# DMAs of the attention exchange and of two stored w2 combinations issued by GpSimd instead of SyncE, and one store moved behind the exchange

## The chip, the cores and the metric

The kernel runs as one program on one core of a Trainium2 chip. The metric is the device time of an execution in microseconds; less is better. Three executions of the kernel before took 1772.20, 1772.83 and 1773.43 us, so the median is 1772.83 us.

## The reference

Three layers follow one another on 2304 tokens of 512 features. Everything is float32.

```python
# 1. attention inside chunks of 64 tokens: 4 batches, 8 heads, 576 tokens, 64 features a head
scores = (q_c @ k_c^T) / 8;  attn = softmax(scores);  x = attn @ v_c      # x: [2304, 512]
# 2. a mixture of 8 dense experts, weighted by a gate that is normalised 8 times by rows and columns
P = exp(x @ w_gate - max);  8 times: P /= row sums;  P /= column sums;  P *= 2304 / 8
out = sum over e of P[:, e] * (relu(x @ w1[e]) @ w2[e])                   # w1[e]: [512, 1024]
# 3. an MLP with three up projections
h = max(out @ w1, out @ w2, out @ w3)                                     # 512 -> 768
result = h @ w_out                                                        # 768 -> 512
```

## The kernel before

The tokens are cut into 18 tiles of 128, and these into three super-blocks of six tiles. A matrix product is done by a scheme of Strassen's kind: seven products of 384 columns stand for eight, and every operand is split into a high and a low part, so that a product is six matmuls. ACT casts the high part; POOL or DVE subtracts it to get the low part (`hilo`, L272 and L273).

**Items.** The work is a list of items. Items 0 to 31 are the mixture's layer on the first super-block: item n is a slice of 256 hidden units, with its own up weights (w1) and down weights (w2), which it reads raw from HBM, combines and splits (`prep`, `prep_x`). The later items take the combined weights back from HBM, where items 0 to 31 have stored them (`keep`: `w1s` for the up weights, `w2s` for the down weights). So only items 0 to 31 issue the DMAs that the change touches, and they end about 570 us into the span.

Inside an item the code walks through seven positions, one for each product (`up`), and hangs the other work on them: `at(n, pos, ...)` registers a step, `early` one that comes ahead of the rest. Each engine runs its instructions in the order in which they are written; nothing is reordered.

**What item n does to the w2 weights.** `prep(n, 2)` casts the raw tile `sw` and splits one half (L273, 128x512, into `wr`). `prep_x` makes two combinations on DVE (L193 to L197). The first, x, is cast by ACT (L203) and completed by DVE (L210); the second, y, is cast by ACT and its low part is subtracted by POOL (L272, L273 into the tile `w2y`). Up to item 14 x and y have one buffer each, in use by every item; later the items alternate between two (`w2z`). So the cast of item n's y waits until the store of item n-1's y has landed. `keep(n, 2)` stores x (L221) and `keep(n, 3)` stores y (L223), 512 KB each, in item n+1 at position 0. That makes 64 such stores.

**The exchange.** Items 1 to 13 also carry the attention of the last twelve tiles. Scores (L804) are matmuls at position 0 of an item; their softmax follows, DVE transposes blocks of 32 (L865, tile `eT`), and `att_swap` (L869) completes the transpose: ACT copies `eT` to `aT` (L872), then four DMAs of 32 partitions and 32 KB exchange blocks between partitions (L876). In the next item PE multiplies `aT` by v (L905, tile `xp`) right behind the next scores, and between them in some items the gate (L922). That makes 48 such DMAs.

**POOL** has in each item: four sums for the next item's up weights (`ws`, L128 to L131), their low parts (L273: 128x768 and 128x1024 into `wr`), the low part of the item's own w2 (128x512), that of y (128x512), and one of the hidden values (`hr`, L301).

**SP** issues every DMA of the kernel before, in the written order. Where an instruction waits, what is behind it waits too.

Of the kernel before, what the change touches and what calls it, by code (L numbers as in the profile page):

```python
# [33 lines left out]
NPAIR = E * F // 256  # L34
# [18 lines left out]
def kernel(ctx: ExitStack, tc: tile.TileContext, qk, vv, wg, wts, wts2, out):  # L53
    nc = tc.nc
# [55 lines left out]
    def own(n):  # L110

        return n < NPAIR

    def raw1(n):
        if n <= NPAIR:
            g = n % NPAIR
            st[n] = rp.tile([P, 4, 256], F32, name="st", tag="st", bufs=2)
            nc.sync.dma_start(out=st[n][:, 1:3].rearrange("p i f -> p (i f)"), in_=wts[2 * g, :, 0])
            nc.sync.dma_start(out=st[n][:, 0::3], in_=wts[2 * g + 1, :, 0].rearrange("p (i f) -> p i f", i=2))

    def raw2(n):
        if own(n):
            sw[n] = rp.tile([P, 2, 512], F32, name="sw", tag="sw")
            nc.sync.dma_start(out=sw[n], in_=wts[2 * n:2 * n + 2, :, 1].rearrange("c p d -> p c d"))

    def strassen_w(v, s, eng):
        tt = eng.tensor_tensor
        tt(out=s[0], in0=v[0], in1=v[3], op=ALU.add)  # L128
        tt(out=s[1], in0=s[0], in1=v[1], op=ALU.subtract)
        tt(out=s[2], in0=v[1], in1=v[0], op=ALU.subtract)  # L130
        tt(out=s[3], in0=v[2], in1=s[1], op=ALU.subtract)  # L131

    sums, sw2 = {}, {}
# [7 lines left out]
    def prep_sums(n):  # L141
        s = sums[n] = rp.tile([P, 4, 256], F32, name="ws", tag="ws")
        strassen_w([st[n][:, i] for i in range(4)], [s[:, i] for i in range(4)], nc.gpsimd)
# [29 lines left out]
    def prep_x(n, step):  # L173

        if not own(n):
            return
        q = lambda c, a: sw[n][:, c].rearrange("p (f a k r) -> p a k f r", a=2, k=2, f=4)[:, a]
        o = lambda x: x.rearrange("p (k f r) -> p k f r", k=2, f=4)
        tt = nc.vector.tensor_tensor
        if step == 0:  # L180
            if n:
                p = wk.tile([P, 2, 256], F32, name="xw", tag="wk")
            else:
                p = ar[:, TS - 2].rearrange("p (a b) -> p a b", a=2)
            s = rp.tile([P, 2, 256], F32, name="w2c", tag="w2c")
            sw2[n] = (p, s)
            for a in range(2):
                nc.scalar.copy(out=o(p[:, a]), in_=q(0, a))
        elif step == 1:
            p, s = sw2[n]  # L190
            w = w2b(n)[:, 0:2]
            if n:
                tt(out=w[:, :, 1], in0=p, in1=w[:, :, 0].bitcast(F32), op=ALU.subtract)  # L193
            tt(out=o(s[:, 0]), in0=q(1, 1), in1=o(p[:, 1]), op=ALU.add)
            tt(out=o(p[:, 1]), in0=q(0, 0), in1=o(p[:, 1]), op=ALU.subtract)
            tt(out=p[:, 0], in0=s[:, 0], in1=p[:, 0], op=ALU.subtract)
            tt(out=o(s[:, 1]), in0=q(1, 0), in1=o(p[:, 0]), op=ALU.subtract)  # L197
            sw.pop(n)
        elif step == 2:
            p, s = sw2[n]  # L200
            x = w2x(n)
            sums["x", n] = x
            nc.scalar.copy(out=x[:, :, 0], in_=p)  # L203
            y = w2z[0][:, 2:4] if w2z and n % 2 else rp.tile([P, 2, 2, 256], F32R, name="w2y", tag="w2y")
            sums["y", n] = y
            hilo(y[:, :, 0], y[:, :, 1], s)
        else:
            p, s = sw2.pop(n)
            x = sums["x", n]
            tt(out=x[:, :, 1], in0=p, in1=x[:, :, 0].bitcast(F32), op=ALU.subtract)  # L210

    def keep(n, step):
        f32 = lambda x: x.bitcast(F32).rearrange("p s h f -> p s (h f)")
        w2o = w2s[n // 2, :, :, n % 2] if own(n) else None
        if step == 0:
            nc.sync.dma_start(out=w1s[n % NPAIR], in_=f32(w1b(n)))
        elif step == 1:
            nc.sync.dma_start(out=w2o[:, 0:1], in_=f32(w2b(n)[:, 0:1]))
            nc.sync.dma_start(out=w2o[:, 5:7], in_=f32(w2b(n)[:, 2:4]))
        elif step == 2:  # L220
            nc.sync.dma_start(out=w2o[:, 2:4], in_=f32(sums.pop(("x", n))))  # L221
        else:
            nc.sync.dma_start(out=w2o[:, 1:5:3], in_=f32(sums.pop(("y", n))))  # L223


    chunks, slot_of = [], {}
# [44 lines left out]
    def hilo(h, l, v, eng=None):  # L271
        nc.scalar.copy(out=h, in_=v)  # L272
        (eng or nc.gpsimd).tensor_tensor(out=l, in0=v, in1=h.bitcast(F32), op=ALU.subtract)  # L273
# [237 lines left out]
    def fold_all():  # L511
        jobs = [(e, t) for e in (0, NRAW - 1, *range(1, NRAW - 1)) for t in range(TS)]
        loads = [j for j in jobs if j[0] != NRAW - 1]
        got = {}

        def load():
            if loads and len(got) < 6:
                e, t = loads.pop(0)
                got[e, t] = big[0].tile([P, DM], F32, name="u", tag="ld", bufs=6)
                nc.sync.dma_start(out=got[e, t], in_=up_part[e, t])  # L520

        for _ in range(5):
            load()
        yield
        for e, t in jobs:
            load()
            if e == 0:
                nc.scalar.activation(out=ar[:, t], in_=got.pop((e, t)), func=AF.Copy, scale=Pt[:, t, e:e + 1])
            else:
                u = spare[0][:, t] if e == NRAW - 1 else got.pop((e, t))  # L530
                nc.vector.scalar_tensor_tensor(out=ar[:, t], in0=u, scalar=Pt[:, t, e:e + 1],
                                               in1=ar[:, t], op0=ALU.mult, op1=ALU.add)
            yield
# [6 lines left out]
    def x_load(k):  # L540
        kind, sb = phases[k]
        if k == 1:
            xf = spare[0].rearrange("p t d -> p (t d)").rearrange("p (i a w) -> p i a w", a=2, w=W)
            T = lambda i: (xf[:, (1, 3, 4, 6).index(i)] if i in (1, 3, 4, 6) else
                           big[0].tile([P, 2, W], F32, name=f"xf{i}", tag=f"xf{i}"))
        else:
            T = lambda i: bg_[:, :7 * 2 * W].rearrange("p (i a w) -> p i a w", a=2, w=W)[:, i]
        xst.update({i: T(i) for i in range(7)})
        for i, (q, h) in {5: (1, 0), 0: (0, 0), 2: (1, 1), 1: (0, 1)}.items():
            for j in range(TS // 2):  # L550
                t, o = sb * TS + 2 * j + q, xst[i][:, :, j * P:(j + 1) * P]
                nc.sync.dma_start(out=o, in_=(xs if kind == "M" else ys)[t, :, 2 * h:2 * h + 2])
                yield
# [314 lines left out]
    def att_swap(t):  # L868
        eT = et_t.pop(t)  # L869
        aT = ap_.tile([P, 2, H, 32], F32, name="aT", tag="aT")  # L870
        at_t[t] = aT
        nc.scalar.copy(out=aT, in_=eT)  # L872
        for c in range(2):
            for i in range(2):
                src, dst = 64 * c + 32 * i, 64 * c + 32 * (1 - i)
                nc.sync.dma_start(out=aT[dst:dst + 32, i], in_=eT[src:src + 32, 1 - i])  # L876

    def raw_of(t):
        if t // 2 not in raw_t:
# [121 lines left out]
    def at(n, pos, fn):  # L1001
        bg.setdefault((n, pos), []).append(fn)

    for m in range(NT - NPE):
        t, n = NPE + m, 1 + m
        at(n, 1, lambda t=t: (att_norm(t), att_T(t)))
        if m:
            early[n, 2] = lambda t=t: att_swap(t)
        else:
            at(n, 2, lambda t=t: att_swap(t))  # L1010
        at(n + 1, 2, lambda t=t: x_save(t))
    for n in range(1, NT - NPE + 3):
        early[n, 0] = lambda n=n: att_slot(n)
    n = NT - NPE + 2
# [3 lines left out]
    for i in range(SINK_ITERS):  # L1018
        a = 7 * (n + 1 + i // 2)
# [43 lines left out]
    at(n, 0, att_close)  # L1063
    for g in range(NPAIR):
        for s_, (a, b) in enumerate(((0, 2 * (0 < g <= NT - NPE)), (0, 6) if g else (1, 0), (1, 0), (1, 0))):
            if (g, s_) != (1, 0):
                at(g + a if g or s_ else NPAIR, b, lambda g=g, s_=s_: keep(g if g or s_ else NPAIR, s_))
    decs, folds = [decode_all(i) for i in range(2)], fold_all()

    def decode_step(n):  # L1070
# [9 lines left out]
    for k in range(1, 4):  # L1080
        n0 = first_of[k]
        g = x_load(k)
# [6 lines left out]
        for pos in range(7):  # L1089
            a = 7 * (n0 - 1) + (pos + 1 if k == 1 else (0, 1, 2, 7, 7, 7, 8)[pos])  # L1090
            b = 7 * (n0 - 1) + (pos + 2 if k == 1 else (1, 2, 3, 7, 7, 8, 9)[pos])
# [3 lines left out]
    for k in (4, 5):  # L1095
        for j in range(TS // 2):
            n = first_of[k - 1] + 3 * j
            if k == 4 and j < 2:
                n = first_of[3] + 3 + j
# [17 lines left out]
    with tc.manual_schedule():  # L1117
# [60 lines left out]
                next(xg)  # L1178
        for product in part[3:]:
            product()  # L1180
        keep(1, 0)
        raw1(2)
        next(xg)
        w2 = w2_first()
# [12 lines left out]
        prep_x(0, 0)  # L1197
        prep_x(0, 1)
        raw2(1)
        prep_sums(2)  # L1200
        prep_x(0, 2)
        prep_x(0, 3)
        hps.close()
        psum = lambda name, n: pool(name, n, space=bass.MemoryType.PSUM, reuse_waits="tile")
# [110 lines left out]
```

## Time and profile before

| | |
|---|---|
| median of three runs | 1772.83 us |
| the profiled execution | 1774.31 us, its span 1772.5 us |
| PE busy | 1761.9 us (99%) |
| DVE, ACT, POOL busy | 1298.8, 777.1 and 997.5 us |
| chain that ended last | PE 94%, DMA 2%, DVE 1%, ACT 1%, issue 1% |
| granted TensorE clock | 1.0 in all 40 slices |
| DMA queues that moved data | one for all of the kernel's DMAs: 206336 packets, 530.97 MB |

A busy time is the sum over the instructions of an engine. The chain is followed back from the last instruction to what released each step. Times in timelines count from the start of the span. Item 1 begins at 34 us (its scores, L804), item 2 at 53, item 3 at 71, item 4 at 89, item 5 at 107, item 6 at 124 us.

### The profile page before, as it was taken

The page shows a single profiled execution, that of the slowest core. Times are in us where ns is not written, and L with a number is a line of the kernel's source. Part 1 is how long each engine was busy: PE and PEld are TensorE (multiplying, and loading weights), DVE is VectorE, ACT ScalarE, POOL GpSimd, SP SyncE. Part 2 cuts the span into 40 slices and gives each one's busy share as a digit, 9 for nine tenths or more (in the row PEclk, how much of TensorE's full clock was granted, in tenths as well). Part 3 has the DMA queues.
Part 4 walks back from the last instruction along what each step waited for, and adds up shares of the span by engine and source line. Part 5 has one row for each costly group of instructions (what it writes and reads, how often), then busy time and mean ns, then how long its engine had stood idle before and what let it go on. Part 6 is the DMA issues. An engine that isn't in the chain of part 4 may idle for free.

```text
span 1772.5 us, 30171 instructions
## 1 busy us (share of the span) xinstructions
PE 1761.9 (99%) x10764; PEld 1683.4 (95%) x10764; DVE 1298.8 (73%) x2342; ACT 777.1 (44%) x1566; POOL 997.5 (56%) x891
## 2 busy tenths in 40 slices
PE   8999999999999999999999999999999999999999
PEld 7888888998989999999999999999999999999998
DVE  8767667678876787887886887878787766664535
ACT  6665664655555534333333434334333333323221
POOL 4665665767777866666675667576766555000000
PEclk9999999999999999999999999999999999999999
DMA  8999998899988998988889779888988786877662
GB/s 284 317 353 366 340 347 311 321 373 340 357 309 333 334 322 273 333 299 306 279 314 318 257 257 346 306 295 295 318 306 316 265 303 241 283 259 255 243 246 105
DMA packets 206486, 532.89 MB, mean 301 GB/s; under 512 B 16160, under 2 KB 95360, under 8 KB 181248
## 3 DMA queue, kind: packets, MB, share of 16 engines
q1 hardware_dynamic: 206336, 530.97, 84.0%
q8 instruction: 85, 1.39, 0.3%
q14 instruction: 65, 0.53, 0.1%
HBM read 373.31 MB, written 156.02 MB: 299 GB/s over the span
## 4 chain that ended last, share of the span: by engine, by line
PE 94%; DMA 2%; DVE 1%; ACT 1%; issue 1%; POOL 0%; SPq 0%; DVEq 0%; ACTq 0%; POOLq 0%
PE pa L353 28%; PE dn L411 27%; PE dn L469 18%; PE pg L353 14%; PE pb L353 7%; DMA w2s<-w2y 1%; DMA upart<-ar 0%; PE xp L905 0%; PE s L804 0%; DMA qk<-in_qk 0%; PE gp L922 0%; DVE e L830 0%; DVE hs L827 0%; DVE hs L819 0%; DVE nm L818 0%
## 5 line engine op out<-in xcount | busy, mean ns | idle before, releaser
L353 PE MATMUL pa<-xh,wr 128*128 128x384 f32 x1808 | 529.2, 337 | 0.0
L469 PE MATMUL dn<-wr,hr 128*128 128x512 f32 x1476 | 356.2, 392 | 0.0
L353 PEld LDWEIGHTS pa<-xh,wr 128*128 128x128 f32 x1808 | 332.7, 188 | 5.2 <-DVE c L366 0.8
L469 PEld LDWEIGHTS dn<-wr,hr 128*128 128x128 f32 x1476 | 275.4, 188 | 53.9
L353 PE MATMUL pa<-xl,wr 128*128 128x384 f32 x904 | 303.2, 335 | 0.0
L411 PE MATMUL dn<-hr,wr 128*128 128x384 f32 x1344 | 274.8, 335 | 0.0
L353 PE MATMUL pg<-xh,wr 128*128 128x384 f32 x904 | 268.3, 337 | 0.1
L360 ACT COPY s<-pa 128x384 f32<-128x384 f32 x244 | 117.3, 481 | 300.1 <-PE pa L353 276.5
L411 PEld LDWEIGHTS dn<-hr,wr 128*128 128x128 f32 x1344 | 236.9, 188 | 0.1
L366 DVE TENSOR_TENSOR c<-pb,s 128x384 f32<-128x384 f32 x82 | 45.7, 557 | 203.0 <-PE pb L353 180.1
L273 POOL TENSOR_TENSOR hr<-c,hr 128x384 fp32r<-128x384 f32 x96 | 111.1, 1163 | 142.2 <-ACT hr L272 137.0
L411 PE MATMUL dn<-hx,wr 128*128 128x384 f32 x840 | 182.8, 338 | 0.0
L353 PEld LDWEIGHTS pa<-xl,wr 128*128 128x128 f32 x904 | 169.7, 188 | 4.0
L353 PEld LDWEIGHTS pg<-xh,wr 128*128 128x128 f32 x904 | 166.5, 188 | 1.9 <-DVE tq L322 0.4
L353 PE MATMUL pg<-xl,wr 128*128 128x384 f32 x452 | 151.1, 334 | 0.0
L411 PEld LDWEIGHTS dn<-hx,wr 128*128 128x128 f32 x840 | 150.9, 188 | 0.0
L273 POOL TENSOR_TENSOR hr<-tq,hr 128x384 fp32r<-128x384 f32 x128 | 148.4, 1175 | 0.5 <-ACT hr L272 0.5
L353 PE MATMUL pb<-xh,wr 128*128 128x384 f32 x452 | 134.1, 337 | 0.0
L420 DVE TENSOR_TENSOR ar<-dn,ar 128x384 f32<-128x384 f32 x240 | 123.0, 546 | 9.5 <-PE dn L411 9.1
L273 POOL TENSOR_TENSOR hx<-c,hx 128x384 fp32r<-128x384 f32 x60 | 68.8, 1150 | 106.0 <-ACT hx L272 105.5
L411 PE MATMUL dn<-hy,wr 128*128 128x384 f32 x504 | 111.1, 336 | 0.0
L420 DVE TENSOR_TENSOR ax<-dn,ax 128x384 f32<-128x384 f32 x180 | 93.2, 550 | 18.2 <-PE dn L411 18.2
(246 smaller groups left out, 3210.8 us busy)
## 6 DMA issues: line engine op xcount, KB each, us to landing
wr<-w2s SPq DMA_DIRECT2D x80, 1024.0 KB, 6.4
w1s<-wr SPq DMA_DIRECT2D x32, 1792.0 KB, 9.7
wr<-w1s SPq DMA_DIRECT2D x53, 1024.0 KB, 7.2
wr<-w1s SPq DMA_DIRECT2D x58, 768.0 KB, 6.4
w2s<-wr SPq DMA_DIRECT2D x55, 512.0 KB, 6.5
wr<-w2s SPq DMA_DIRECT2D x52, 512.0 KB, 7.1
wr<-scr SPq DMA_DIRECT2D x22, 1024.0 KB, 5.1
wr<-scr SPq DMA_DIRECT2D x27, 768.0 KB, 5.8
```

The costliest lines, as they stand in the source:

```text
L273: (eng or nc.gpsimd).tensor_tensor(out=l, in0=v, in1=h.bitcast(F32), op=ALU.subtract)
L353: nc.tensor.matmul(ps, lhsT=wt[:, x, ws], rhs=y[:, xi, k], start=b not in begun, stop=k == 1 and i == 2, skip_group_check=True)
L360: nc.scalar.copy(out=s[pos], in_=ps)
L366: nc.vector.tensor_tensor(out=inner, in0=ps, in1=s[other], op=ALU.add)
L411: nc.tensor.matmul(p, lhsT=w[:, a, dt * P:(dt + 1) * P], rhs=h[m][:, b], start=m == 0 and q == 0, stop=m == 1 and q == 2)
L420: nc.vector.tensor_tensor(out=o, in0=p, in1=o, op=ALU.add)
L469: nc.tensor.matmul(o, lhsT=h[:, hi, ts], rhs=w, start=(f == 0 and i == 0), stop=(f == 1 and i == 2))
```

## The change

The DMAs of `keep(n, 2)`, `keep(n, 3)` and `att_swap` are issued by GpSimd (POOL) and no longer by SP. The store of item 1's up weights, `keep(1, 0)`, leaves the prologue and is registered like the others, at position 2 of item 1, behind `att_swap`. In the prologue `prep_x(0, 2)`, which casts x and y of item 0 and subtracts y's low part on POOL, comes ahead of `prep_sums(2)`, four sums on POOL.

```diff
--- before.py
+++ after.py
@@ -218,9 +218,9 @@
             nc.sync.dma_start(out=w2o[:, 0:1], in_=f32(w2b(n)[:, 0:1]))
             nc.sync.dma_start(out=w2o[:, 5:7], in_=f32(w2b(n)[:, 2:4]))
         elif step == 2:
-            nc.sync.dma_start(out=w2o[:, 2:4], in_=f32(sums.pop(("x", n))))
+            nc.gpsimd.dma_start(out=w2o[:, 2:4], in_=f32(sums.pop(("x", n))))
         else:
-            nc.sync.dma_start(out=w2o[:, 1:5:3], in_=f32(sums.pop(("y", n))))
+            nc.gpsimd.dma_start(out=w2o[:, 1:5:3], in_=f32(sums.pop(("y", n))))
 
 
     chunks, slot_of = [], {}
@@ -873,7 +873,7 @@
         for c in range(2):
             for i in range(2):
                 src, dst = 64 * c + 32 * i, 64 * c + 32 * (1 - i)
-                nc.sync.dma_start(out=aT[dst:dst + 32, i], in_=eT[src:src + 32, 1 - i])
+                nc.gpsimd.dma_start(out=aT[dst:dst + 32, i], in_=eT[src:src + 32, 1 - i])
 
     def raw_of(t):
         if t // 2 not in raw_t:
@@ -1063,8 +1063,7 @@
     at(n, 0, att_close)
     for g in range(NPAIR):
         for s_, (a, b) in enumerate(((0, 2 * (0 < g <= NT - NPE)), (0, 6) if g else (1, 0), (1, 0), (1, 0))):
-            if (g, s_) != (1, 0):
-                at(g + a if g or s_ else NPAIR, b, lambda g=g, s_=s_: keep(g if g or s_ else NPAIR, s_))
+            at(g + a if g or s_ else NPAIR, b, lambda g=g, s_=s_: keep(g if g or s_ else NPAIR, s_))
     decs, folds = [decode_all(i) for i in range(2)], fold_all()
 
     def decode_step(n):
@@ -1178,7 +1177,6 @@
                 next(xg)
         for product in part[3:]:
             product()
-        keep(1, 0)
         raw1(2)
         next(xg)
         w2 = w2_first()
@@ -1197,8 +1195,8 @@
         prep_x(0, 0)
         prep_x(0, 1)
         raw2(1)
+        prep_x(0, 2)
         prep_sums(2)
-        prep_x(0, 2)
         prep_x(0, 3)
         hps.close()
         psum = lambda name, n: pool(name, n, space=bass.MemoryType.PSUM, reuse_waits="tile")
```

SP's queue from the end of the prologue into item 1, before (`w1s` is the store of item 1's up weights, `st` and `sw` are raw weights, `w2s<-w2y` is the store of y, `aT` the exchange):

```order
L216 DMA w1s<-wr 128x3584
L118 DMA st<-in_wts 128x512
L119 DMA st<-in_wts 128x2x256
L124 DMA sw<-in_wts 128x2x512
L118 DMA st<-in_wts 128x512
L119 DMA st<-in_wts 128x2x256
L790 DMA qk<-in_qk 128x1024
L218 DMA w2s<-wr 128x512
L219 DMA w2s<-wr 128x2x512
L221 DMA w2s<-wr 128x2x512
L223 DMA w2s<-w2y 128x2x512
L876 DMA aT<-eT 32x256 x4
```

and now:

```order
L118 DMA st<-in_wts 128x512
L119 DMA st<-in_wts 128x2x256
L124 DMA sw<-in_wts 128x2x512
L118 DMA st<-in_wts 128x512
L119 DMA st<-in_wts 128x2x256
L790 DMA qk<-in_qk 128x1024
L218 DMA w2s<-wr 128x512
L219 DMA w2s<-wr 128x2x512
L216 DMA w1s<-wr 128x3584
L124 DMA sw<-in_wts 128x2x512
L218 DMA w2s<-wr 128x512
L219 DMA w2s<-wr 128x2x512
```

The store of `w1s` has gone from ahead of the `st` loads to behind the two stores of `w2s<-wr` (item 0's own w2); the x and y stores and the exchange have left the queue, so that the next `sw` load follows at once.

POOL's queue in the same place, before (`ws` are the sums, `wr` the low parts, `hr` the hidden values; the row `wr<-ws` belongs to the up weights of item 2):

```order
L170 TENSOR_TENSOR wr<-sw,wr 128x2x256
L128 TENSOR_TENSOR ws<-st 128x256
L129 TENSOR_TENSOR ws<-ws,st 128x256
L130 TENSOR_TENSOR ws<-st 128x256
L131 TENSOR_TENSOR ws<-st,ws 128x256
L273 TENSOR_TENSOR w2y<-w2c,w2y 128x2x256
L273 TENSOR_TENSOR wr<-st,wr 128x3x256
L273 TENSOR_TENSOR wr<-sw,wr 128x2x256
L301 TENSOR_TENSOR hr<-c,hr 128x384
L273 TENSOR_TENSOR wr<-ws,wr 128x2x2x256
L273 TENSOR_TENSOR w2y<-w2c,w2y 128x2x256
```

and now:

```order
L170 TENSOR_TENSOR wr<-sw,wr 128x2x256
L273 TENSOR_TENSOR w2y<-w2c,w2y 128x2x256
L128 TENSOR_TENSOR ws<-st 128x256
L129 TENSOR_TENSOR ws<-ws,st 128x256
L130 TENSOR_TENSOR ws<-st 128x256
L131 TENSOR_TENSOR ws<-st,ws 128x256
L221 DMA w2s<-wr 128x2x512
L223 DMA w2s<-w2y 128x2x512
L273 TENSOR_TENSOR wr<-st,wr 128x3x256
L273 TENSOR_TENSOR wr<-sw,wr 128x2x256
L876 DMA aT<-eT 32x256 x4
L301 TENSOR_TENSOR hr<-c,hr 128x384
```

The low part of y stands ahead of the four sums; the two stores follow the sums, and the four DMAs of the exchange stand ahead of `hr`. The row that comes next in the changed queue is `wr<-ws`.

POOL's queue in item 4 before, from the low parts of the next up weights to the sums of the item after:

```order
L273 TENSOR_TENSOR wr<-st,wr 128x3x256
L273 TENSOR_TENSOR wr<-ws,wr 128x2x2x256
L273 TENSOR_TENSOR wr<-sw,wr 128x2x256
L273 TENSOR_TENSOR w2y<-w2c,w2y 128x2x256
L301 TENSOR_TENSOR hr<-c,hr 128x384
```

and now:

```order
L273 TENSOR_TENSOR wr<-st,wr 128x3x256
L221 DMA w2s<-wr 128x2x512
L223 DMA w2s<-w2y 128x2x512
L273 TENSOR_TENSOR wr<-ws,wr 128x2x2x256
L876 DMA aT<-eT 32x256 x4
L273 TENSOR_TENSOR wr<-sw,wr 128x2x256
L273 TENSOR_TENSOR w2y<-w2c,w2y 128x2x256
L301 TENSOR_TENSOR hr<-c,hr 128x384
```

Two stores stand between the two low parts of the up weights, and four exchange DMAs between the second of these and the low part of w2.

## Rows read from the trace of the kernel before

**Rows 1.** The page, part 1: busy time, share of span and instructions by engine.

```profile
PE 1761.9 (99%) x10764; PEld 1683.4 (95%) x10764; DVE 1298.8 (73%) x2342; ACT 777.1 (44%) x1566; POOL 997.5 (56%) x891
```

**Rows 2.** Windows: start:end, length, then busy time (instructions) of PE, PEld, DVE, ACT, POOL.

```profile
45.00:60.00 15.00, 13.95 (x141) 12.17 (x140) 10.71 (x24) 10.64 (x22) 13.68 (x12) 1.00 0.94 321
120.00:135.00 15.00, 14.71 (x142) 12.60 (x142) 8.45 (x19) 10.90 (x24) 10.52 (x9) 1.00 1.01 359
195.00:210.00 15.00, 14.60 (x106) 12.70 (x99) 11.98 (x28) 9.71 (x22) 9.40 (x9) 1.00 0.95 352
```

**Rows 3.** Timeline of PE (start, length; in brackets idle before and releaser).

```profile
53.17 0.69 PE L804 MATMUL s<-qk 64*64 64x64 f32 x30 [1.05 <-DVE wr L210]
...
54.37 0.69 PE L905 MATMUL xp<-aT,v 64*64 64x64 f32 x32
...
55.45 0.52 PE L353 MATMUL pg<-xh,wr 128*128 128x384 f32 x2
...
106.63 0.69 PE L804 MATMUL s<-qk 64*64 64x64 f32 x32
107.15 0.71 PE L905 MATMUL xp<-aT,v 64*64 64x64 f32 x32
...
123.64 0.69 PE L804 MATMUL s<-qk 64*64 64x64 f32 x32
```

**Rows 4.** Chain that ended last: start, length, what.

```profile
45.40 5.44 DMA w2s<-w2y
...
113.24 9.27 DMA w2s<-w2y
```

**Rows 5.** Timeline of SP's DMA queue: start, length of the issue.

```profile
29.17 0.42 SPq L216 DMA_DIRECT2D w1s<-wr  x1
...
91.84 0.42 SPq L223 DMA_DIRECT2D w2s<-w2y  x1
...
96.85 2.41 SPq L876 DMA_DIRECT2D aT<-eT  x4
```

**Rows 6.** Timeline of POOL in the prologue and item 1.

```profile
41.18 0.73 POOL L128 TENSOR_TENSOR ws<-st 128x256 f32<-128x256 f32 x1 [4.89 <-DMA st<-in_wts]
...
44.09 1.29 POOL L273 TENSOR_TENSOR w2y<-w2c,w2y 128x512 fp32r<-128x512 f32 x1
...
48.41 1.00 POOL L301 TENSOR_TENSOR hr<-c,hr 128x384 fp32r<-128x384 f32 x1
49.38 2.39 POOL L273 TENSOR_TENSOR wr<-ws,wr 128x1024 fp32r<-128x1024 f32 x1
```

**Rows 7.** Timeline of POOL in item 4.

```profile
92.77 1.85 POOL L273 TENSOR_TENSOR wr<-st,wr 128x768 fp32r<-128x768 f32 x1 [1.60 <-ACT wr L272]
94.58 2.39 POOL L273 TENSOR_TENSOR wr<-ws,wr 128x1024 fp32r<-128x1024 f32 x1
97.94 1.29 POOL L273 TENSOR_TENSOR wr<-sw,wr 128x512 fp32r<-128x512 f32 x1 [0.97 <-ACT wr L272]
103.86 1.30 POOL L273 TENSOR_TENSOR w2y<-w2c,w2y 128x512 fp32r<-128x512 f32 x1 [4.63 <-ACT w2y L272]
```

**Rows 8.** Timeline of POOL in item 26.

```profile
456.37 1.19 POOL L130 TENSOR_TENSOR ws<-st 128x256 f32<-128x256 f32 x1
...
467.93 1.30 POOL L273 TENSOR_TENSOR w2y<-w2c,w2y 128x512 fp32r<-128x512 f32 x1 [3.79 <-ACT w2y L272]
```

**Rows 9.** Timeline of ACT: casts of the second w2 combination for items 0, 4, 5.

```profile
37.99 0.62 ACT L272 CAST w2y<-w2c 128x512 fp32r<-128x512 f32 x1
...
103.16 0.62 ACT L272 CAST w2y<-w2c 128x512 fp32r<-128x512 f32 x1
...
122.53 0.62 ACT L272 CAST w2y<-w2c 128x512 fp32r<-128x512 f32 x1 [0.59 <-DMA w2s<-w2y]
```

**Rows 10.** Tile w2y: landing time of its DMAs.

```profile
DMA to landing us min/median/max: 5.1/7.4/9.3
```

**Rows 11.** Tile aT: landing time of its DMAs.

```profile
DMA to landing us min/median/max: 1.8/4.1/8.7
```


## The prediction

> **What bounds the kernel now.** I read the page first. PE is busy for 1761.9 of 1772.5 us, POOL for 56% [rows 1]. No more than 10.6 us of the span is idle time of PE, and the question is how much of it stands in items 1 to 13, where the moved DMAs are, and hangs on them. The table of windows answers that: in three stretches of 15 us PE is busy for 13.95, 14.71 and 14.60 us [rows 2]. That is 1.05, 0.29 and 0.40 us of idle time, 1.74 us together.
>
> The timeline of PE and the chain of waits then say what ended these waits. At 53.17 us the scores of item 2 had waited 1.05 us for DVE [rows 3]. The chain goes back from there to a store of y issued at 45.40 and landed 5.44 us later; ACT's cast of the next y, behind which other ACT and DVE work is queued, could not start before that [rows 4]. The window at 120 us has the same cause: the store issued at 113.24 landed after 9.27 us [rows 4], so that item 5's cast ran at 122.53, 1.11 us ahead of the next scores at 123.64, where item 4's ran at 103.16, 3.47 us ahead of 106.63 [rows 3, 9]. It was 2.36 us late and PE lost 0.29 us, so a late cast is free up to some 2.07 us. I take the third window for a repetition of the second, four items on.
>
> So the upside is 1.74 us, 0.1%. A measurement of this kernel cannot tell a change below 0.2%, or 3.5 us, from none.
>
> **What a DMA on POOL costs POOL.** No row shows one. The lower end is the same issue on SP: 0.42 us for a store of y, and 2.41 us for four DMAs of the exchange, 0.60 each [rows 5]. The upper end is the longest POOL instruction here, 2.39 us [rows 6, 7]. Nothing excludes either end, though a gain for POOL is excluded, since it issues nothing now. I take what POOL needs for a tile of that shape: 1.30 us for each of two stores (its 128x512 row [rows 7]) and 0.73 us for each of four exchange DMAs (its 128x256 row [rows 6], the smallest tile in it). An item then gets 2 x 1.30 + 4 x 0.73 = 5.5 us, between 3.2 and 14.3.
>
> **Items 2 to 12.** POOL's own work in an item is four sums of 0.73, then 1.85, 2.39, 1.29, 1.30 and 1.00, so 10.8 us [rows 6, 7]. Two starts of scores without a late store are 17.8 us apart (three items from 53.17 to 106.63), the shortest item 17.0 [rows 3]. POOL's idle time is thus 6.2 to 7.0 us. In item 4 it has 0.97 us ahead of the low part of w2 and 4.63 us ahead of that of y, which waits for ACT [rows 7]: 5.60 us against the 5.5 needed. The order is: first low part to 94.6, stores at 94.6 and 95.9, second low part from 97.2 to 99.6, exchange from 99.6 to 102.5, low part of w2 to 103.8, and y's at 103.86 as before. So nothing behind them starts later. What is late is the DMAs:
> - y's store starts at 95.9 where SP had it at 91.84 [rows 5]. With the median landing of 7.4 us it is there at 103.3, with the longest of 9.3 at 105.2 [rows 10]. ACT wants it at 103.16 and may have it 2.07 us later, at 105.2. So PE does not wait, with nothing to spare in the worst case.
> - the last exchange DMA starts at 101.8 where SP began the four at 96.85 [rows 5]. With the median landing of 4.1 us [rows 11] it is there at 105.9; PE wants it at 107.15 [rows 3].
>
> In the item of the second stall the store starts hardly earlier than before (113.4 for 113.24), but no longer behind SP's loads in one queue. With the median landing it is there at 120.8 and not at 122.5. I take the second and the third stall as gone: -0.69 us.
>
> **Item 1.** It is the tightest. SP no longer sends 1792 KB at 29.17 ahead of the raw weights [rows 5], for whose landing POOL's sums waited until 41.18 [rows 6]; at the 321 GB/s of the nearest window [rows 2] that is up to 5.6 us. The swapped order lets y's low part (1.29) start when its cast ends, at 38.61 [rows 9], so the sums run from 39.9 to 42.8, 1.3 us earlier than now. Then come the stores to 45.4 (y's from 44.1, 1.3 us earlier than now), low parts of 1.85 and 1.29 to 48.5, the exchange to 51.5, the hidden values to 52.5 and the second low part of item 2's up weights to 54.9. It now starts at 49.38 and ends at 51.8 [rows 6]. Without the stall of 1.05 us PE would want the exchange at 53.3 and that low part at 54.4 [rows 3]. The last exchange DMA starts at 50.7 and lands between 52.5 and 54.8 (shortest 1.8, median 4.1 [rows 11]); the low part is 0.5 us late. A wait of 0 to 1.5 us, in place of one of 1.05, which itself shrinks by up to 1.3 but competes with the 1792 KB that now start around 41. I put the old stall and the new one equal: 0, with -1.05 and +1.5 as its ends.
>
> **Items 13 to 31.** Only two stores an item are added. POOL is idle for 3.79 us ahead of y's low part [rows 8], against 2 x 1.30 = 2.6. The buffers of x and y alternate from item 15 on, so that a landing has an item more. Cost 0. SP's shorter queue gains nothing here: the windows without an idle PE have nothing to give back.
>
> **The sum.** -0.69 + 0 + 0 = -0.7 us. The profiled execution took 1774.31 us, 1.8 us more than its span, and would take 1773.6. At the median of the runs, 1.5 us below it, that is 1772.83 - 0.7 = 1772.1 us. Its own range is 1770.9 (all three stalls gone, and noise) to 1776.3 (the bound of a measurable difference).
>
> **Rivals.**
> - POOL becomes the bound of items 1 to 12. From six DMAs of more than 6.2 to 7.0 us together it is late by a bit more in every item, and PE waits for the exchange first, which has 1.2 us to spare. Midway between the ends of a store, 1.4 us a DMA, the sum is 8.4: 8.4 - 6.6 = 1.8 us in each of 11 items, 20 us, so 1792 us. At the upper end it is 14.3 - 6.6 = 7.7 us x 11 and (4.8 - 3.8) x 19, or 1876 us. For it: nothing in the trace bounds the issue from above. Against it: SP does the same in a third of the time taken here for a store. Chance 0.26.
> - POOL's DMAs are stretched by DVE's work beside them. One of the sums takes 1.19 us in item 26 [rows 8] where it takes 0.73 in item 1; DVE is busy for 11 of 15 us in the stretch of item 1 [rows 2]. With 0.46 us more on each of six DMAs the sum is 5.5 + 2.8 = 8.3 us, 1.7 us over the idle time in 11 items: 19 us, 1791 us. Against it: the other POOL rows of items 1 to 4 are not stretched. Chance 0.08. The Trainium skill has such a rule ("SBUF — State Buffer", section "SBUF: two separate sides"): the descriptors of a DMA issued from GpSimd are written by GpSimd's own cores, which an instruction of VectorE in a two-port mode locks out of the port that they share. The page excepts TENSOR_TENSOR from these modes (section "Who interferes with whom"), which most rows of DVE are. No run here shows it, and by it the time would be this rival's.
> - The stores land no faster than now, at 9.3 us at worst: the second and third stall stay, and item 1 gives back what it takes. 1772.8 to 1773.3 us, chance 0.06. The Trainium skill holds with that ("DMA: Bandwidth & Descriptors", section "Issuing engines are not separate DMA queues"): DMAs of all issuing engines run on the same 16 DMA engines and interleave, and only the issuer's time is saved. The trace agrees so far as these engines are the limit, at a busy share of 0.94 to 1.01 in the three windows of rows 2.
> - Item 1's stall goes too: -1.74 us, 1771.1 us, chance 0.12. Faster than that by 1.8 us or more would need idle time that PE does not have there: 0.03.
>
> **How the numbers follow.** The forecast has 0.45. With the third and fourth rival it makes no measurable difference: 0.63. Slower by over 0.2% are the first two: 0.34. Faster: 0.03. The range reaches up to 1792, the middle prices of the first two, and leaves out about half of them, 0.15, and 0.03 below 1770.6.
>
> **What would show it.** Right: POOL's DMA rows near 1.3 and 0.7 us; no idle PE at the items around 124 and 195 us; some idle time left around 53; y's low part still ended by its wait for ACT. Wrong: POOL without idle time ahead of y's low part in items 2 to 12, PE waiting for `aT` or for a low part by POOL at every item, or casts of y later than 2 us.

## The result, and the profile after

The changed kernel takes 1798.2 us (median of 4 runs, 1797.89 to 1799.47), the kernel before 1772.69 us (4 runs). The ratio is 1.0143, 95% interval [1.013, 1.0155]: 25.5 us slower, outside the predicted range. In the experiments below before's median lies between 1773.2 and 1774.3 us, so ratios are compared, not times across groups.

The page of the changed kernel, part 1 (answers to [rows 1]), and the rows of its DMA queues:

```profile
PE 1772.9 (99%) x10764; PEld 1690.8 (94%) x10764; DVE 1306.7 (73%) x2342; ACT 776.4 (43%) x1566; POOL 1060.7 (59%) x1003
...
q1 hardware_dynamic: 186624, 495.84, 77.7%
q0 software_dynamic: 10752, 35.13, 5.0%
```

The span grew from 1772.5 to 1797.7 us, by 25.2 us. PE's busy time grew by 11.0 us with the same number of instructions, so PE worked slower in places; the other 14.2 us are idle time of PE. POOL got 63 us more work and is busy for no more than 59%.

The stretches of 15 us that answer to [rows 2] (start:end, length, busy time of PE, PEld, DVE, ACT, POOL, then granted clock, DMA share, GB/s), with the one that follows the third:

```profile
45.00:60.00 15.00, 9.40 (x77) 8.23 (x79) 5.38 (x12) 8.12 (x17) 11.58 (x13) 0.93 1.01 401
120.00:135.00 15.00, 13.38 (x72) 11.76 (x71) 5.79 (x12) 6.32 (x13) 8.19 (x9) 1.00 1.00 377
195.00:210.00 15.00, 15.00 (x107) 13.20 (x109) 6.97 (x16) 7.60 (x15) 8.98 (x9) 1.00 1.01 378
210.00:225.00 15.00, 12.02 (x92) 10.26 (x92) 7.94 (x18) 10.30 (x23) 12.43 (x14) 0.89 0.94 361
```

PE is idle for 5.6 us in the first, 1.6 in the second, 3.0 in the last. The chain of waits of the changed kernel names what was late, in four places (start, length, what; answers to [rows 4]):

```profile
44.74 11.76 DMA w2s<-w2y
...
121.78 13.41 DMA w2s<-w2y
...
198.06 12.77 DMA w2s<-w2y
...
272.26 10.39 DMA w2s<-w2y
```

These are stores of y, in items 1, 5, 9 and 13. Their landing is the new thing. Over the tile w2y, and over aT (answers to [rows 10, 11]):

```profile
DMA to landing us min/median/max: 4.6/7.4/13.4
DMA to landing us min/median/max: 2.5/6.2/10.8
```

The median of y's store is what it was; the longest went from 9.3 to 13.4 us. x's store (L221), issued 0.75 us ahead of y's, goes the same way: 8.5 us at the longest before, 12.5 now. Around the second place stand, on SP's queue and on POOL's of the changed kernel (start, length of the issue):

```profile
120.66 0.38 SPq L911 DMA_DIRECT2D xs<-xr  x1
121.09 0.42 SPq L216 DMA_DIRECT2D w1s<-wr  x1
128.26 0.38 SPq L124 DMA_DIRECT2D sw<-in_wts  x1
```

```profile
121.03 0.75 POOL L221 DMA_DIRECT2D w2s<-wr  x1
121.78 0.74 POOL L223 DMA_DIRECT2D w2s<-w2y  x1
122.54 2.42 POOL L273 TENSOR_TENSOR wr<-ws,wr 128x1024 fp32r<-128x1024 f32 x1
124.89 2.02 POOL L876 DMA_DIRECT2D aT<-eT  x4
```

The 1792 KB store of the up weights (`w1s`, L216) starts 0.69 us ahead of y's. In the other three places it starts 2.66 us ahead (42.08), 0.37 behind (198.43) and 0.80 ahead (271.46). Before, it stood behind y's store and the exchange, 6.9 us later than y's in this item (120.12 against 113.24 [rows 4]). ACT then waits, and behind it PE. From the timelines of ACT and of PE:

```profile
133.58 0.58 ACT L203 CAST wr<-xw 128x512 fp32r<-128x512 f32 x1 [6.87 <-DMA w2s<-wr]
135.22 0.62 ACT L272 CAST w2y<-w2c 128x512 fp32r<-128x512 f32 x1 [1.05 <-DMA w2s<-w2y]
```

```profile
58.78 1.12 PE L804 MATMUL s<-qk 64*64 64x64 f32 x30 [5.60 <-DVE wr L210]
...
134.95 0.69 PE L804 MATMUL s<-qk 64*64 64x64 f32 x30 [1.62 <-DVE wr L210]
...
137.72 1.61 PE L905 MATMUL xp<-aT,v 64*64 64x64 f32 x32 [1.51 <-ACT ar L482]
```

The first of the ACT rows waits for x's store, which landed 12.5 us after its issue at 121.03, the second for y's. The kernel before waited in this item too, for y's store 0.59 us [rows 9] and for x's:

```profile
121.35 0.59 ACT L203 CAST wr<-xw 128x512 fp32r<-128x512 f32 x1 [3.99 <-DMA w2s<-wr]
```

So ACT stands still for 6.87 and 1.05 us where it stood for 3.99 and 0.59. The first of the PE rows answers to the first of [rows 3]: a wait of 5.60 us for 1.05, and the 30 matmuls behind it take 1.12 us and not 0.69. Windows of 2 us around it show why (columns as above):

```profile
54.00:56.00 2.00, 0.00 (x0) 0.00 (x0) 0.00 (x0) 0.58 (x1) 0.00 (x0) 1.00 1.03 390
56.00:58.00 2.00, 0.00 (x0) 0.00 (x0) 0.43 (x1) 1.47 (x4) 0.78 (x1) 0.95 1.05 391
58.00:60.00 2.00, 1.22 (x34) 1.10 (x38) 1.34 (x4) 1.26 (x4) 1.92 (x4) 0.50 0.92 342
60.00:62.00 2.00, 2.00 (x49) 1.47 (x45) 1.55 (x4) 0.27 (x1) 1.35 (x2) 0.50 0.35 101
62.00:64.00 2.00, 2.00 (x7) 2.00 (x8) 0.95 (x4) 1.94 (x5) 0.00 (x0) 0.50 0.75 237
64.00:66.00 2.00, 2.00 (x9) 1.66 (x9) 1.79 (x5) 1.43 (x2) 1.96 (x2) 0.85 1.02 402
```

After 5.6 us without a matmul the granted clock is 0.50, the lower of the two levels (1.2 of 2.4 GHz), and comes back some 7 us later. Two more such stretches lie at 136 and 215 us, behind the stalls there. The windows of 15 us with a lower clock are 45 and 60 us (0.93, 0.85), 135 us (0.77) and 210 us (0.89): what is lacking to 1.00 in them comes to 8.4 us, most of the 11.0 us by which PE was busy longer. In another, from 0 to 15 us (0.89), ahead of the first moved DMA, PE is busy 0.8 us longer than before.

Last, POOL in item 4 (answers to [rows 7]). The DMA issues were cheaper than I took them:

```profile
102.76 0.75 POOL L221 DMA_DIRECT2D w2s<-wr  x1
103.51 0.74 POOL L223 DMA_DIRECT2D w2s<-w2y  x1
104.27 2.43 POOL L273 TENSOR_TENSOR wr<-ws,wr 128x1024 fp32r<-128x1024 f32 x1
106.61 2.02 POOL L876 DMA_DIRECT2D aT<-eT  x4
108.65 1.30 POOL L273 TENSOR_TENSOR wr<-sw,wr 128x512 fp32r<-128x512 f32 x1
111.95 1.30 POOL L273 TENSOR_TENSOR w2y<-w2c,w2y 128x512 fp32r<-128x512 f32 x1 [1.99 <-ACT w2y L272]
```

0.75 + 0.74 + 2.02 = 3.5 us in an item, and POOL is still idle ahead of y's low part, waiting for ACT. POOL is not the bound.

### The profile page after: what moved, and what is told of

The parts are those of the page before. It is cut to its first block, busy times and chain, and to the rows that moved or that the text cites. A ratio compares the mean times of both kernels' runs of the same rounds, so it can differ in the third digit from the quotient of the medians.

```text
span 1797.7 us, 30202 instructions
## 1 busy us (share of the span) xinstructions
PE 1772.9 (99%) x10764; PEld 1690.8 (94%) x10764; DVE 1306.7 (73%) x2342; ACT 776.4 (43%) x1566; POOL 1060.7 (59%) x1003
## 4 chain that ended last, share of the span: by engine, by line
PE 90%; DVE 3%; DMA 3%; POOL 1%; issue 1%; ACT 1%; SPq 0%; POOLq 0%; DVEq 0%; ACTq 0%
PE pa L353 26%; PE dn L411 26%; PE dn L469 16%; PE pg L353 14%; PE pb L353 7%; DMA w2s<-w2y 3%; PE xp L905 0%; DMA qk<-in_qk 0%; PE s L804 0%; POOL w2y L273 0%; POOL wr L273 0%; DVE hr L304 0%; DVE ar L484 0%; DVE wr L193 0%; DVE hs L827 0%
```

## The experiments

For each kernel I also read by how much ACT's first w2 cast of an item (L203) starts later than in the kernel before, in us. In the four runs with the change or a part of it:

| item | changed | e10 | e14 | e1 |
|---|---|---|---|---|
| 2 | +8.1 | +1.3 | +7.8 | +0.1 |
| 6 | +14.9 | +0.6 | +14.6 | -0.3 |
| 10 | +19.5 | -0.1 | +20.3 | -1.1 |
| 14 | +21.0 | -0.1 | +21.7 | -0.3 |
| 18 | +25.0 | +3.9 | +21.7 | +3.8 |
| 30 | +24.8 | +3.7 | +21.7 | +3.6 |

The losses come in steps, where the late stores are, and in a last one between items 14 and 18, where none of them is waited for. (About 1 us of the first step is there before the first moved DMA; over all runs this start varies by -0.7 to +1.8.)

**Which part of the change: e1 to e4.** One part alone, or all but one:

```diff
# e1: of the change, only the stores of x and y (keep, L221 and L223)
+            nc.gpsimd.dma_start(out=w2o[:, 2:4], ...)
+            nc.gpsimd.dma_start(out=w2o[:, 1:5:3], ...)
# e2: only the exchange (L876)
+                nc.gpsimd.dma_start(out=aT[dst:dst + 32, i], ...)
# e3: only keep(1, 0) out of the prologue, and prep_x(0, 2) ahead of prep_sums(2)
# e4: e1 and e2 together, with the prologue of before
```

> Only the stores of x and y go to POOL's queue; the exchange stays on SP, and the prologue is that of before. Theory (y's store, now issued by POOL later in the item and beside SP's loaded queue, lands late and holds ACT's next cast): the loss is in the stores, so 1785 to 1800 us, with landings of y of 11 us or more and ACT waiting for them. Rival A (the exchange on POOL is what costs): 1773 us, within 3 us. Rival B (the prologue's edits cost): 1773 us, within 3 us.

Measured: 1778.88 us, ratio 1.003 [1.0018, 1.0042]. Less than the theory said, more than its rivals.

> Only the exchange goes to POOL's queue; the stores stay on SP, and the prologue is that of before. Theory (the stores): 1770 to 1776 us, y's landing at most 10 us. Rival A (the exchange): 1785 to 1800 us, PE waiting for aT or for a low part that POOL makes behind it. Rival B (the prologue): 1773 us, within 3 us.

Measured: 1774.34 us, 1.0004 [0.9994, 1.0013]: nothing.

> Only the prologue's edits (the store of item 1's up weights moved behind item 1's start, x's low part ahead of the raw sums); all DMAs stay on SP. Theory (the stores): on SP's one queue y's store stays ahead of the up weights' store, so 1770 to 1776 us. Rival A (the exchange): the same. Rival B (the prologue): item 1 loses its 7 us here too, 1779 us or more.

Measured: 1773.71 us, 1.0 [0.9991, 1.0009]: nothing.

> The changed kernel with the prologue of before: stores and exchange on POOL's queue, the up weights of item 1 stored in the prologue again. Theory (the stores): items 5, 9 and 13 lose what they lost; item 1, whose 1792 KB no longer start beside y's store, loses less: 1786 to 1796 us. Rival A (the exchange) the same. Rival B (the prologue): 1773 us, within 3 us.

Measured: 1796.28 us, 1.0126 [1.0111, 1.0141], 0.3 us above the theory's range. Here item 1's cast is in time again (+0.0 us), but the exchange issued in it lands late, and PE waits for `aT` twice at the start of item 2 (1.37 and 0.82 us).

So no part alone does it: stores 0.3%, exchange 0.04%, both 1.26%. A late issue of y by POOL isn't enough, since in e1 POOL issues it as late (95.39, 10.4 us behind the first w2 cast of its item, where the changed kernel has 103.51, 10.2 us behind). What e1 keeps is the exchange on SP. There SP waits for DVE's transposed `eT`, and the 1792 KB behind it start 6.6 us after y's store (101.96). With both moved nothing holds SP, and they start beside it. That became the theory; the next runs were to break it.

**The 1792 KB: e5 to e8.**

```diff
# e5: changed kernel, the up weights' store on POOL too, behind the exchange
-            nc.sync.dma_start(out=w1s[n % NPAIR], ...)
+            nc.gpsimd.dma_start(out=w1s[n % NPAIR], ...)
# e6: kernel before, keep(g, 0) of items 2 to 12 registered at (g, 0), ahead of x and y
+    for g in range(2, NT - NPE + 1):
+        at(g, 0, lambda g=g: keep(g, 0))
# e7: changed kernel, keep(g, 0) at position 5 of items 1 to 12
-... ((0, 2 * (0 < g <= NT - NPE)), ...
+... ((0, 5 * (0 < g <= NT - NPE)), ...
# e8: changed kernel, keep(g, 2) and keep(g, 3) at position 6 of item g (from item 1 on)
-... (0, 6) if g else (1, 0), (1, 0), (1, 0)
+... (0, 6) if g else (1, 0), (0, 6) if g else (1, 0), (0, 6) if g else (1, 0)
```

> The changed kernel with the up weights' store (1792 KB) issued by POOL too, behind the exchange, so that it stands behind y's store again as it did on SP's queue. Theory now (with both the stores and the exchange gone, SP no longer waits between the items and sends the 1792 KB beside or ahead of y's store, which then lands late): 1773 to 1781 us, landings of y at most 11 us, no wait of PE for DVE's L210 over 1.5 us. Rival L (y's store is late because POOL issues it behind its sums, whoever is beside it): 1790 us or more. Rival Q (a DMA on POOL's queue lands slowly by itself): 1790 us or more.

Measured: 1801.45 us, 1.0157 [1.0142, 1.0172].

> The changed kernel with the 1792 KB store of items 1 to 12 later on SP's queue, behind the next item's raw down weights. Theory now: it no longer starts beside y's store, 1773 to 1785 us; the upper part if the later store keeps the buffer of the up weights busy and POOL's or ACT's next parts wait for it. Rivals L and Q: 1790 us or more.

Measured: 1801.66 us, 1.0159 [1.0144, 1.0175]. Both runs missed the theory's numbers, but neither asked its question cleanly: the store that was pushed back now holds the buffer of the up weights. The waits of ACT in e5, then in e7 (engine, line, what it waited for: us, times, longest):

```profile
ACT wr L272 <- DMA w1s<-wr: 46.2, 12, 6.8
ACT wr L203 <- DMA w2s<-wr: 20.0, 7, 4.3
```

```profile
ACT wr L272 <- DMA w1s<-wr: 39.5, 11, 6.4
ACT wr L203 <- DMA w2s<-wr: 23.6, 8, 5.5
```

The first of each is new: the changed kernel has none. What e5 does show is that POOL's queue is not slow in itself. With the 1792 KB behind them, the stores of y (L223) land in 5.2 us in the median and 9.9 at the longest; from SP's queue, before, it was 7.1 and 9.3. And item 1's loss is gone in both runs: item 2's cast is 0.6 us later than before in e5 and 0.4 us earlier in e7.

> The kernel before, all on SP, with the 1792 KB store of items 2 to 12 put ahead of the stores of x and y instead of behind the exchange. Theory now: the harm comes without POOL's queue, 1778 to 1798 us, landings of y of 11 us or more. Rivals L and Q: 1773 us within 3 us, since y's store is issued by SP, at most 1 us later than before.

Measured: 1781.65 us, 1.0041 [1.0026, 1.0056]; the longest landing of y 12.1 us. POOL's queue is not in this kernel: the 1792 KB ahead of y's store, on SP alone, do harm of the same kind.

> The changed kernel with POOL issuing the stores of x and y at the end of their item, ahead of the next raw sums and not behind them (some 5 us earlier); the 1792 KB stay where they are on SP. Theory now: y's store is ahead of the 1792 KB by several us again, 1773 to 1779 us. Rival L (lateness): the same, 1773 to 1779 us. Rival Q (slow landing on POOL's queue): 1785 us or more, landings of 11 to 13 us still there.

Measured: 1783.02 us, 1.0049 [1.0032, 1.0066], above the range. Item 0's y keeps its place in this edit, so that item 1's wait is still there (PE 5.47 us for L210). In items 2 to 13 ACT no longer waits for a store.

**The order itself: e9 to e12.** e9 and e10 leave y's store late and change what starts beside it, without holding the up weights' buffer longer. e11 is the control of e10, and e12 has the early stores of e8 without its stall in item 1.

```diff
# e9: e4, but the first of the four exchange DMAs on SP
+                (nc.gpsimd if c or i else nc.sync).dma_start(out=aT[...], ...)
# e10: changed kernel, 256 of the 1792 KB in items 1 to 13 (e11: the same in the kernel before);
# the other 1536 KB are left out, and the later reads take other items' weights
+            k = 1 if 1 <= n <= 13 else 7
+            nc.sync.dma_start(out=w1s[n % NPAIR, :, 0:k], in_=f32(w1b(n)[:, 0:k]))
# e12: e8 with the prologue of before
```

> Stores and exchange on POOL's queue with the prologue of before, but the first of the four exchange DMAs stays on SP, so that SP waits there for DVE's transposed probabilities as it did before, and the 1792 KB behind it start as late as before. Theory (SP, no longer held, sends the 1792 KB beside y's store): 1775 to 1782 us, as with the stores alone. Rival H (it is the exchange on POOL's own queue that, together with the stores, is too much for POOL or lands late): 1791 to 1797 us, since three of its four DMAs are still there.

Measured: 1783.29 us, 1.0055 [1.004, 1.007]. One DMA of 32 KB put back on SP, which makes SP wait, takes back more than half of what e4 lost. In item 5 of e9 y's store, issued at 116.33, lands in 8.9 us, where it took 13.1 in e4. SP's queue there:

```profile
117.50 0.52 SPq L876 DMA_DIRECT2D aT<-eT  x1
118.07 1.30 SPq L911 DMA_DIRECT2D xs<-xr  x1
119.41 0.93 SPq L216 DMA_DIRECT2D w1s<-wr  x1
```

It ends 1 us above the theory's range: item 2 still waits 2.19 us for `aT`, and the last step (items 14 to 18) is there in full (+4.1 us).

> The changed kernel, but of the up weights' store of items 1 to 13 only the first 256 of 1792 KB are sent, from the same place (the later reads of these weights take those of other items, which are as large). Theory: what lands beside y's store is short, 1772 to 1780 us, landings of y in items 1 to 13 at most 9 us. Rival L (y's store is late because POOL issues it late): 1790 us or more, the stalls of items 5 and 9 still there.

Measured: 1777.38 us, 1.0026 [1.0015, 1.0036]. Nearly all of the loss ahead of item 14 is gone (table). The landing of y in items 1 to 13 is at most 8.7 us, although POOL issues it as late as ever.

> The kernel before with the same shortened store of the up weights, as the control of that edit: both say 1770 to 1773.5 us, since PE has only 1.7 us to get back; anything below would mean that the shortened store is worth something by itself.

Measured: 1773.59 us, 1.0004 [0.9995, 1.0014], 0.1 us above the range, beside a before of 1773.25 us. The shorter store is worth nothing by itself.

> Stores ahead of POOL's raw sums, exchange on POOL, and the prologue of before, so that no 1792 KB stand ahead of item 1's store of y. Theory: item 1's stall of 5.5 us and the slow clock behind it go, 1773 to 1778 us. Rival (what the early stores left, 9 us, is the price of POOL's queue as such): 1781 to 1785 us.

Measured: 1779.21 us, 1.0033 [1.002, 1.0046], 1 us above the range. Item 1's wait is gone; a wait of 2.0 us for `aT` is left, and the last step in part.

One more comparison needs no further run. In item 13, which has no exchange, these kernels too issue y's store and the 1792 KB within 1 us of each other. Where y's store stood ahead of them on the same queue (before, e2, e3, e5, e6), it landed in 4.9 to 6.6 us; where it was issued 0.3 us ahead of them on the other queue (e1, e13), in 10.3 and 8.2 us. Here being first counted on one queue and did little on two.

**The step of items 14 to 18: e13 to e17.** It stands in e1, e9 and e10 alike. The trace of e1 has at that place, on POOL and on DVE:

```profile
284.94 0.72 POOL L223 DMA_DIRECT2D w2s<-w2y  x1
285.69 2.42 POOL L273 TENSOR_TENSOR wr<-ws,wr 128x1024 fp32r<-128x1024 f32 x1
288.06 1.28 POOL L273 TENSOR_TENSOR wr<-sw,wr 128x512 fp32r<-128x512 f32 x1
```

```profile
286.63 0.31 DVE L968 TENSOR_REDUCE rs<-Pp 128x18 f32<-128x144 f32 x1
286.97 2.42 DVE L969 TENSOR_SCALAR rs<-rs 128x18 f32<-128x18 f32 x1
289.43 0.27 DVE L970 RECIPROCAL rs<-rs 128x18 f32<-128x18 f32 x1
```

An addition of a constant to 18 numbers takes 2.42 us, from the middle of one POOL subtraction to the end of the next (289.34). In the kernel before the same instruction falls between the two and takes 0.18 us; the issues of x and y have pushed POOL's work over it. Over its 8 executions L969 has (shortest/median/longest ns) before, and then changed:

```profile
L969 DVE TENSOR_SCALAR rs<-rs x8: 176/179/706, 281.1 to 335.5; 128x18 f32<-128x18 f32 x8
```

```profile
L969 DVE TENSOR_SCALAR rs<-rs x8: 250/1278/2723, 302.0 to 358.6; 128x18 f32<-128x18 f32 x8
```

DVE's low parts of the hidden values are behind it, and PE waits for them. In the changed kernel, behind its L969 rows:

```profile
319.22 0.44 PE L353 MATMUL pg<-xh,wr 128*128 128x384 f32 x1 [0.86 <-DVE hr L304]
...
336.09 0.44 PE L353 MATMUL pg<-xh,wr 128*128 128x384 f32 x1 [0.50 <-DVE hr L304]
...
369.96 0.44 PE L353 MATMUL pg<-xh,wr 128*128 128x384 f32 x1 [0.88 <-DVE hr L304]
```

These idle times are 2.2 us together; the rest of the step of 4 us shows in no idle time of PE. A fourth wait of this kind, 0.62 us at 285.30, is ahead of the first L969 row and stays in e14.

The remedy that I tried rests on another row: L980, also a TENSOR_SCALAR of DVE in these items, reads PSUM and takes 153 to 167 ns in every one of these kernels. So the row sums were put into PSUM, in spare columns of the tile that is there:

```diff
# e13: e1 with it; e14: changed kernel; e15: kernel before; e16: e13 with the stores early as in e8; e17: e10 with it
-        nc.vector.tensor_reduce(out=rs, in_=p, axis=AX.X, op=ALU.add)
-        nc.vector.tensor_scalar_add(out=rs, in0=rs, scalar1=EPS)
+        nc.vector.tensor_reduce(out=Pp[1], in_=p, axis=AX.X, op=ALU.add)
+        nc.vector.tensor_scalar_add(out=rs, in0=Pp[1], scalar1=EPS)
```

> As the stores alone (e1), but the row sums to which L969 adds its constant stand in PSUM and not in SBUF; nothing else is changed. Theory S (POOL's sums, shifted by the DMA issues, hold this DVE instruction, DVE's low parts come late and PE waits in items 14 to 17): L969 takes 0.2 us throughout, the lag of items 14 to 17 (3.6 us) goes, 1774 to 1776.5 us. Rival (the remaining lag is the price of the stores' landing or of POOL's time for the issues): 1778 to 1780 us, with DVE's low parts as late as in e1.

Measured: 1775.14 us, 1.0008 [0.9999, 1.0017]. The instruction takes 176 to 177 ns in all 8 executions, and four of them lie inside a POOL subtraction of 2.4 us (the first at 287.18, in one from 285.89 to 288.31). The lag of items 14 to 18 is 0.0 us.

> The changed kernel with the row sums in PSUM. Theory S: the two causes add, so that only the lag of items 14 to 17 goes, 3 to 5 us, 1793 to 1796 us. Rival: 1798 us, within 2 us.

Measured: 1794.65 us, 1.011 [1.0094, 1.0125]. The last step is gone, the others are all there (table): the two causes add.

> The kernel before with the row sums in PSUM, as control: its held L969 rows (0.3 and twice 0.7 us) lie beside an idle DVE and cost PE nothing, so both say 1772 to 1775 us.

Measured: 1774.25 us, 1.0001 [0.9992, 1.001].

> The stores of x and y on POOL's queue ahead of the raw sums, the exchange on SP, the prologue of before, the row sums in PSUM: y's store is early and neither the 1792 KB nor L969 is in the way. Theory: 1771 to 1775 us, no measurable difference from before, since PE has only 1.7 us to give back. Rival (stores on POOL's queue cost something in themselves): 1777 us or more.

Measured: 1774.73 us, 1.0004 [0.9995, 1.0013]. In items 1 to 13 y's store lands up to 10.8 us after its issue, later than in any item of the kernel before, and ACT waits no more than 0.7 us for one: early and slow does no harm.

> The changed kernel with both taken away: the up weights' store of items 1 to 13 cut to 256 KB (the later reads take other items' weights), and the row sums in PSUM. Theory (these two are all of the loss): 1773 to 1776 us, within 0.15% of before. Rival (the two stores and the exchange on POOL's queue cost something more): 1777 us or more.

Measured: 1774.51 us, 1.0003 [0.9994, 1.0012]. With both causes taken away the changed kernel is the kernel before. No version beat the kernel before by what can be measured.

## Why the prediction was wrong

**The step that failed** is the one for items 2 to 12: "With the median landing of 7.4 us it is there at 103.3, with the longest of 9.3 at 105.2 [...]. So PE does not wait, with nothing to spare in the worst case." For the item of the second stall it goes on: "no longer behind SP's loads in one queue. With the median landing it is there at 120.8 and not at 122.5." The start there was right (113.4 forecast; 121.78 measured, in an item that was by then 8 us late); the landing, taken as 7.4 us, was 13.41. From item 2 on the landing times came from a queue in which the 1792 KB stood behind y's store (item 1's were sent 16 us ahead of it). I counted what is queued behind the moved DMAs on POOL, and asked of SP only what its shorter queue could gain. I did not ask what SP sends earlier once it no longer waits for `eT`. The answer was the largest store of the item. Beside it y's landing is up to 13.4 us. In item 5 y's cast ran 12.7 us later than before, over 4 us more than the delay with which that item began, and it had been 2.36 us late before, where the text had 2.07 us to spare. The sum had no term at all for x's store, which lands as late and holds ACT first (6.87 us), as it did before (3.99 us). e10 takes this neighbour away and e9 puts SP's wait back; e6 does harm of the same kind with SP alone. By the table items 2 to 13 lose some 13 of the 25 us in this way, and some 20 with item 1, the slow clock included.

**Late start and neighbour together.** I had the later start of y's store right (10.2 us behind its item's first w2 cast for the y that is stored in item 4, where SP issued it 7.0 us behind). It used up the slack, as the text said; alone it cost nothing to the items before 14 (e1, e13). With the row sums in PSUM either remedy was enough: no large neighbour (e17), or an earlier start (e16, which also leaves the exchange on SP; with the exchange on POOL, e12 keeps a lag of 1.2 us ahead of item 14).

**Item 1**, priced at -1.05 to +1.5 us, lost about 7. The text had the 1792 KB "that now start around 41" compete with y's store, and gave that no price (its one price for them, 5.6 us at 321 GB/s, comes to 5.7, and stands for the time that they no longer take ahead of the raw weights). The estimate was there to be made: x, y, `w1s` and item 0's own w2, 512 + 512 + 1792 + 768 KB, were issued within 4.5 us; at the 321 GB/s that the text used there 3.67 MB take 11.4 us, against 5.44 us that y's store had before and 11.76 that it took.

**A stall was priced at its own length.** The lower clock behind the three long ones added 3.3, 3.5 and 1.7 us.

**Items 13 to 31 at 0** failed by 4 us. The rival "DVE stretches POOL's DMAs" was of the right kind and had the wrong direction: no DMA row of POOL is stretched in these items (0.73 us each; only two of the sums are, up to 1.45 us, as they were before), but POOL's subtractions hold an instruction of DVE. The Trainium skill has that side too, on the same page ("SBUF — State Buffer", section "Who interferes with whom"): when a TENSOR_SCALAR of VectorE in a two-port mode and GpSimd meet, one of them blocks fully, and which of them is decided by issue order. The rows agree with the block, and it outlasts the POOL subtraction that was running: it ends with the next one. That PSUM operands stay out of it is in the Trainium skill too ("VectorE: DVE Perf Modes", section "Why PSUM operands drop a tier": a two-port mode needs both SBUF read ports, and VectorE has one for PSUM); e13 agrees, with 176 to 177 ns throughout. The prediction had asked only what DVE does to POOL, not the reverse.

**What held.** POOL hid the issues: 3.5 us an item where I took 5.5, at 0.74 us a store for 1.30 and 0.50 us an exchange DMA for 0.73. With that the first rival (POOL as the bound) falls. The range did reach to 1792 us, for that wrong reason. The rival "the stores land no faster than now, at 9.3 us at worst" fell with its bound; the rule of the Trainium skill beside it ("DMA: Bandwidth & Descriptors", section "Issuing engines are not separate DMA queues") held: DMAs of all issuing engines run on the same DMA engines and interleave. The rows agree: in item 9 y's store was issued 0.37 us ahead of SP's 1792 KB and landed after 12.77 us.

**What stays open.** Why the exchange's landing costs item 2 about 2 us in e4, e9 and e12 was not tried; the text had counted on its median of 4.1 us there, not on the longest of 8.7 [rows 11]. Nor was why just items 1, 5, 9 and 13 are hit. In the other items y's store is issued 3.3 us or more behind the 1792 KB, or 1.7 us or more ahead of them (103.51 against 105.39), and lands in 5.4 to 8.9 us. The trace of the changed kernel shows what precedes: in items 4, 8 and 12 SP stops for the stores `upart` (L486; the last at 113.35), and what waited behind them goes out at once. In item 5 that is 4096 KB from SP between 115.31 and 121.51, the 1792 KB among them; for item 6 the same DMAs are spread over 12 us. When y's store was issued, 4352 KB were under way in item 5 and 2304 in item 6. That this burst is what picks the items is argued, not tried.

## What to carry to other kernels

A DMA that waits on its queue is also what keeps those behind it back. Before moving it to another queue, write down what the old queue will send instead, how large that is, and whose landing it will share the engines with; a landing time read from the old order does not hold in the new one, and being first on another queue is not being first on the same one. Check as well which small instructions of another engine the moved issues push into each other, and price a stall of the bound engine at more than its length where its clock falls behind it.

## What the runs showed of the hardware

- Issuing a DMA costs POOL 0.72 to 0.75 us for a store of 512 KB (0.87 for the first) and 0.50 us for one of 32 KB over 32 partitions; from POOL's queue a store of 512 KB lands in 5.2 us (median, e5) where the 1792 KB stand behind it on the same queue.
- A store of 512 KB that is issued 0.3 us ahead of one of 1792 KB lands in 8.2 to 10.3 us when the two are on different queues (e1, e13, item 13); up to 0.9 us ahead of it on one queue it lands in 4.9 to 6.6 us.
- A TENSOR_SCALAR of DVE on 128x18 elements in SBUF took up to 2.74 us beside POOL's subtractions, past the end of one and to the end of the next; with its source in PSUM 0.18 us.
- After 5.6 us without a matmul TensorE's granted clock stood at 0.50 for some 7 us.
